# Loading the last four w2 blocks as 112 lines over all engines and 16 lines over four of them

## The chip, the cores and the metric

One core of a Trainium2 chip runs the whole program. The metric is device time in microseconds (us) per execution, the median of several. A profile of one execution comes with each kernel; its times count from the start of its span, which is 1.2 to 1.4 us shorter than the device time.

Throughout, a *line* is one of the 128 partitions of the on-chip memory, and an *engine* without a name is one of the 16 DMA engines. The trace gives them no numbers; where a text names engines 0 to 3, 0 and 1 or 1, or says how many lines each engine carries, that is the author's assumption.

## The reference, cut to what matters

A decoding step of a transformer block with a batch of 2: modulation from `c @ w_mod`, attention of 32 heads over caches of 32768 keys and values, then an MLP. The kernel moves 178 MB of weights and caches through the core once. The argument here touches only the last product, `h @ w2`:

```python
    def _B_ref(x, w1, b1, w2, b2):
        y = _layernorm(x, axis=-1)
        h = _gelu(jnp.einsum('bsd,df->bsf', y, w1) + b1)
        return jnp.einsum('bsf,fd->bsd', h, w2) + b2          # w2: 3584 x 1024, bf16
    ...
    h = _layernorm(x, axis=-1) * (1 + cb) + sb
    x = x + gb * _B_ref(h, B_w1, B_b1, B_w2, B_b2)
    return x
```

## The kernel before

All large loads are one stream on the sync queue, issued as far ahead as memory is free. The 3584 rows of w2 are 28 blocks of 128 rows, one row per line; a block is 2 KB on each line. They come in five loads. Blocks 16 to 27 are the stationary operand of 8 matmuls each, which add into one PSUM tile; the result follows after two small vector operations, a transposing matmul and a copy.

```python
W2_ITEMS = ((0, 8, 96), (8, 16, 112), (16, 24, 128), (24, 27, 144), (27, 28, 150))  # first, end, offset in KB
... # cut
    w2_v = B_w2.rearrange("(p j) n -> p j n", j=FT)
    for m, (j0, j1, off) in enumerate(W2_ITEMS):
        add(("w2", m), [j1 - j0, DM], w2_v[:, j0:j1, :], off * KB)      # 128 lines each
... # cut
    for g in range(16, FT):
        m, j = w2_of[g]
        it = need("w2", m)
        for k in range(KT8):
            pe(lambda e, ...: e.matmul(psO[:, 2 * k:2 * k + 2], lhsT=w[:, j, k * 128:(k + 1) * 128], rhs=gT[:, g, 0:2],
                                       start=False, stop=(g == FT - 1), skip_group_check=True),
               reads=[it.reg, "gT"], writes=["psO"], ...)
    dve(...)   # times the modulation, plus the residual; then one matmul, one copy, the store
```

## Time and profile before

| kernel before | value |
|---|---|
| device time, median of 6 | 420.06 us (419.93 to 420.28) |
| profiled span | 418.7 us |
| DMA busy on its main queue | 98.8% of 16 engines' span |
| blocks 16 to 23 landed (last of 16 completions) | 413.23 us |
| blocks 24 to 26 landed | 415.12 us |
| block 27 landed | 415.76 us |
| last matmul of block 27 starts | 416.02 us |

The trace has several completions per load: 16 for each load of w2 in the kernel before, and 1, 2, 4, 1 and 8 for the bias loads of 1, 2, 4, 1 and 8 lines. The author reads them as one per engine that took part, so that the spread between them tells how far apart the engines are. One further line of the kernel before is needed later. It is the stretch from 411.2 to 415.2 us: length, busy time of PE, PEld, DVE, ACT and POOL with counts, granted clock, DMA busy share, GB/s.

```profile
411.20:415.20 4.00, 3.67 (x73) 3.50 (x74) 0.00 (x0) 0.00 (x0) 0.00 (x0) 0.50 0.80 330
```

DMA engines were busy for 80% of these 4 us and moved 330 GB/s: a fifth of their time was idle, as some had run out of work (seven completions of block 27, the last load of w2, were in by 414.49).

### The profile page before, as it was taken

The numbers are of one execution on the slowest core, as the hardware profiler recorded it, in microseconds if no ns is written. First come the engines' busy times: TensorE is split into PE (matmuls) and PEld (weight loads), VectorE is DVE, ScalarE is ACT, GpSimd is POOL, SyncE is SP. The second block draws the span as 40 slices with busy tenths as digits, with TensorE's granted clock in tenths as the row PEclk, the third lists the DMA queues.
The fourth block names the chain that finished last, engine by engine and source line by source line (L and its number), as shares of the span: only waits on it lengthen the run. The fifth ranks groups of instructions, "written<-read, shape, count | busy, mean of one in ns | idle before, by whom it ended". The sixth has DMA issues, their size and how long they took to land.

```text
span 418.7 us, 11609 instructions
## 1 busy us (share of the span) xinstructions
PE 291.0 (70%) x5183; PEld 231.3 (55%) x5183; DVE 209.6 (50%) x423; ACT 149.4 (36%) x179; POOL 6.8 (2%) x29
## 2 busy tenths in 40 slices
PE   1407449766996895699369957976995699564536
PEld 1104219762993794299149926962894399221214
DVE  1201105546677676467726664766477567620411
ACT  2000015533565364256405632643365166400100
POOL 3000000000000000000000000000000000000000
PEclk9999557986896997799589958986697889576585
DMA  9989999999999999999999999999999999899995
GB/s 373 450 380 449 448 404 493 398 406 446 441 432 429 423 451 429 419 454 457 391 435 476 407 416 448 438 438 426 438 438 426 416 460 457 377 448 428 424 427 249
DMA packets 5581, 178.42 MB, mean 426 GB/s; under 512 B 698, under 2 KB 706, under 8 KB 964
## 3 DMA queue, kind: packets, MB, share of 16 engines
q1 hardware_dynamic: 5572, 178.28, 98.8%
q8 instruction: 8, 0.13, 0.1%
q14 instruction: 1, 0.01, 0.0%
HBM read 178.28 MB, written 0.00 MB: 426 GB/s over the span
## 4 chain that ended last, share of the span: by engine, by line
DMA 71%; PE 24%; DVE 2%; issue 1%; ACT 1%; SPq 1%
DMA V<-in_A_v_cache_dram 39%; DMA wo<-in_A_wo_dram 10%; DMA K<-in_A_k_cache_dram 10%; PE psZ L584 10%; DMA w<-in_B_w_dram 9%; PE psKT L536 8%; DMA wmod<-in_w_mod_dram 4%; PE psS L548 1%; PE psZ L548 1%; PE psS L655 1%; PE psZ L729 1%; PE psZ L469 1%; ACT KT_sb L540 0%; PE psS L469 0%; DVE m1c L553 0%
## 5 line engine op out<-in xcount | busy, mean ns | idle before, releaser
L536 PE MATMUL psKT<-ident,K 128*128 128x128 bf16 x2048 | 163.1, 229 | 11.5 <-DMA K<-in_A_k_cache_dram 11.5
L540 ACT ACTIVATE KT_sb<-psKT 128x1024 bf16<-128x1024 bf16 x96 | 98.2, 1025 | 124.4 <-PE psKT L536 124.4
L542 DVE COPY KT_sb<-psKT 128x1024 bf16<-128x1024 bf16 x160 | 106.7, 688 | 61.6 <-PE psKT L536 61.2
L536 PEld LDWEIGHTS psKT<-ident,K 128*128 128x128 bf16 x2048 | 126.7, 102 | 13.0 <-DMA K<-in_A_k_cache_dram 12.7
L584 PE MATMUL psZ<-V,E_sb 128*32 128x512 bf16 x512 | 46.4, 541 | 23.2 <-DMA V<-in_A_v_cache_dram 20.0
L548 PE MATMUL psS<-qcur,KT_sb 128*128 128x8 bf16 x1024 | 44.7, 167 | 2.2 <-issue 2.2
L584 PEld LDWEIGHTS psZ<-V,E_sb 128*32 128x32 bf16 x512 | 18.7, 130 | 47.7 <-issue 38.8
L548 PE MATMUL psZ<-qcur,KT_sb 128*128 128x8 bf16 x1024 | 43.0, 167 | 2.2 <-issue 1.5
L548 PEld LDWEIGHTS psS<-qcur,KT_sb 128*128 128x128 bf16 x1024 | 40.0, 97 | 2.3 <-issue 2.3
L548 PEld LDWEIGHTS psZ<-qcur,KT_sb 128*128 128x128 bf16 x1024 | 37.9, 96 | 3.4 <-issue 1.6
L572 ACT ACTIVATE E_sb<-S_sb 128x512 bf16<-128x512 f32 x32 | 19.5, 630 | 29.6 <-DVE S_sb L570 29.6
L570 DVE TENSOR_TENSOR S_sb<-S_sb,gmb 128x512 f32<-128x512 f32 x32 | 20.0, 685 | 0.3
L576 DVE TENSOR_REDUCE rs<-E_sb 128x8 f32<-128x512 bf16 x32 | 19.7, 675 | 0.0
L469 PE MATMUL psS<-wmod,inT 128*32 128x512 bf16 x32 | 5.1, 624 | 16.2 <-DMA wmod<-in_w_mod_dram 16.2
L553 DVE TENSOR_REDUCE m1c<-psZ 128x8 f32<-128x512 f32 x16 | 11.1, 693 | 10.2 <-ACT S_sb L552 10.1
L595 DVE RECIPROCAL rinv<-psM 128x1 f32<-128x1 f32 x8 | 1.3, 168 | 27.7 <-PE psM L593 27.7
L605 PE MATMUL psM<-msum,hmat 128*128 128x128 f32 x16 | 4.2, 347 | 13.3 <-DVE msum L600 13.3
L559 PE MATMUL psM<-identf,m 128*8 128x128 f32 x16 | 4.3, 369 | 13.1 <-DVE m L556 13.1
L553 DVE TENSOR_REDUCE m1c<-psS 128x8 f32<-128x512 f32 x16 | 11.1, 693 | 3.2 <-ACT S_sb L552 3.1
L552 ACT ACTIVATE S_sb<-psZ 128x512 f32<-128x512 f32 x16 | 9.5, 595 | 7.5 <-PE psZ L548 7.5
L477 DVE COPY S_sb<-psS 128x512 f32<-128x512 f32 x1 | 0.7, 690 | 22.9 <-PE psS L469 22.9
L469 PEld LDWEIGHTS psS<-wmod,inT 128*32 128x32 bf16 x32 | 1.1, 132 | 19.3 <-DMA wmod<-in_w_mod_dram 18.0
(123 smaller groups left out, 167.5 us busy)
## 6 DMA issues: line engine op xcount, KB each, us to landing
K<-in_A_k_cache_dram SPq DMA_DIRECT2D x16, 4096.0 KB, 27.1
wq<-in_A_wq_dram SPq DMA_DIRECT2D x2, 4096.0 KB, 44.8
wo<-in_A_wo_dram SPq DMA_DIRECT2D x2, 4096.0 KB, 39.0
w<-in_B_w_dram SPq DMA_DIRECT2D x2, 3584.0 KB, 32.5
wmod<-in_w_mod_dram SPq DMA_DIRECT2D x1, 6144.0 KB, 29.8
w<-in_B_w_dram SPq DMA_DIRECT2D x3, 2048.0 KB, 37.8
wmod<-in_w_mod_dram SPq DMA_DIRECT2D x1, 4608.0 KB, 15.8
wmod<-in_w_mod_dram SPq DMA_DIRECT2D x1, 1536.0 KB, 6.0
```

Source lines behind the costliest of these rows:

```text
L469: pe(lambda e, w=it.view, k=k, kk=kk, ch=ch, n=n, q=q: e.matmul(bank[n][32 * q:32 * q + 32, :], lhsT=inT[:, k, :], rhs=w[:, kk, ch * 512:( ...
L536: pe(lambda e, kq=kq, jj=jj, w=kt, t=t: e.transpose(psKT[kq][:, jj * 128:(jj + 1) * 128], w[:, t, :], ident[:, :]), reads=[it.reg, "ident" ...
L540: act(lambda e, src=src: e.activation(KT_sb[g8][:, :, :], src, ACT.Copy), reads=[f"psKT{kq}"], writes=[f"KT_sb{g8}"], sem=f"ev{cc}_{g8}")
L542: dve(lambda e, src=src: e.tensor_copy(KT_sb[g8][:, :, :], src), reads=[f"psKT{kq}"], writes=[f"KT_sb{g8}"], sem=f"ev{cc}_{g8}")
L548: pe(lambda e, t=t, jj=jj: e.matmul(ps[:, t * HPG:(t + 1) * HPG], lhsT=KT_sb[g8][:, jj, :], rhs=qcur[:, :], start=True, stop=True), reads= ...
L552: act(lambda e: e.activation(Sc, ps.rearrange("p (t h) -> p h t", h=HPG), ACT.Copy), reads=[preg], writes=[f"S_sb_{cc}"], sem=f"sc{cc}")
L553: dve(lambda e: e.tensor_reduce(m1c[:, :, cc], ps.rearrange("p (t h) -> p h t", h=HPG), AX.X, ALU.max), reads=[preg], writes=[f"m1c{cc}"])
L559: pe(lambda e: e.matmul(psM[0:HPG, 0:128], lhsT=m1[:, :], rhs=identf[:, :], start=True, stop=True), reads=["m1", "identf"], writes=["psM"])
L570: dve(lambda e: e.tensor_tensor(Sc, Sc, gmb[:, :].unsqueeze(2).to_broadcast([128, HPG, TPC]), ALU.subtract), reads=[f"S_sb_{cc}", "gmb"], ...
L572: act(lambda e: e.activation(Ec, Sc.rearrange("p h (u t) -> p u h t", t=4), ACT.Exp, scale=SCALE), reads=[f"S_sb_{cc}"], writes=[f"E_sb_{c ...
L576: dve(lambda e: e.tensor_reduce(rs4[:, :, cc], Ec.rearrange("p u h t -> p h u t"), AX.XY, ALU.add), reads=[f"E_sb_{cc}"], writes=[f"rs4_{c ...
L584: pe(lambda e, t4=t4, tg=tg, q=q: e.matmul(psO[32 * q:32 * q + 32, :], lhsT=E_sb[:, tg // 4, :, :].rearrange("p h t -> p (h t)"), rhs=vt[: ...
```

## The change

At the end of the stream seven or eight of the 16 engines finish 1.3 us ahead of the rest. In the kernel before, the packets of the eight instruction fetches lasted 881 to 960 ns each, and after the sixth, seventh and eighth of them six, seven and eight completions of a load came about 1.3 us behind the early ones, to the end of the run. The change wants to hand four engines more lines and all others fewer. The last four blocks are loaded with 112 lines; that each engine then carries 7 instead of 8 is the author's count. The remaining 16 lines, with all four blocks (8 KB per line), come as five small loads of 4, 4, 4, 2 and 2 lines.

```diff
-W2_ITEMS = ((0, 8, 96), (8, 16, 112), (16, 24, 128), (24, 27, 144), (27, 28, 150))
+W2_ITEMS = ((0, 8, 96), (8, 16, 112), (16, 24, 128))
+W2_END = ((24, 27), (27, 28))
+W2_LINES = 112
+W2_REST = ((112, 116), (116, 120), (120, 124), (124, 126), (126, 128))
+W2_AT = 144
 ...
+    j0 = W2_END[0][0]
+    w2e = nc.alloc_sbuf_tensor_at("w2e", [128, FT - j0, DM], BF16, offset=abase + W2_AT * KB)
+    for m, (l0, l1) in enumerate(W2_REST):
+        add(("w2r", m), [FT - j0, DM], w2_v[l0:l1, j0:FT, :], W2_AT * KB, slot="w2r", view=w2e[l0:l1, :, :])
+    for m, (ja, jb) in enumerate(W2_END):
+        add(("w2e", m), [jb - ja, DM], w2_v[0:W2_LINES, ja:jb, :], (W2_AT + 2 * (ja - j0)) * KB, view=w2e[0:W2_LINES, ja - j0:jb - j0, :])
 ...  # the loads of w2 no longer wait for one another, as the last ones share a buffer (cut)
 ...  # the matmuls of blocks 24 to 27 read w2e and wait for its load and for the five small ones
```

More of the change, by code (lines that the diff above doesn't have):

```diff
@@ L333, in bass_adaLN_cond__gqa_block_cached__mixer_channel_mlp__decode_kernel, with add @@
     KB = 1024
-    def add(key, shape, src, off, slot=None):
+    def add(key, shape, src, off, slot=None, view=None):
         it = Item()
@@ L341, in add @@
         it.sem = f"d_{slot or it.reg}"
-        it.view = views.get(slot)
+        it.view = views.get(slot) if view is None else view
         if it.view is None:
@@ L383, in need @@
             cur = stream[pos[0]]
-            old = [o.reg for o in stream[:cur.n] if o.off < cur.off + cur.nbytes and cur.off < o.off + o.nbytes]
+            old = [o.reg for o in stream[:cur.n] if not (o.key[0][:2] == cur.key[0][:2] == "w2") and o.off < cur.off + cur.nbytes and cur.off < o.off + o.nbytes]
             if len(cur.view.shape) == 3:
@@ L725, in bass_adaLN_cond__gqa_block_cached__mixer_channel_mlp__decode_kernel @@
     for g in range(16, FT):
-        m, j = w2_of[g]
-        it = need("w2", m)
+        if g in w2_of:
+            m, j = w2_of[g]
+            it = need("w2", m)
+            w, regs = it.view, [it.reg]
+        else:
+            m = 0 if g < W2_END[0][1] else 1
+            it = need("w2e", m)
+            w, j, regs = w2e, g - W2_END[0][0], [it.reg] + [by_key["w2r", n].reg for n in range(len(W2_REST))]
         for k in range(KT8):
-            pe(lambda e, w=it.view, g=g, j=j, k=k: e.matmul(psO[:, 2 * k:2 * k + 2], lhsT=w[:, j, k * 128:(k + 1) * 128], rhs=gT[:, g, 0:2],
+            pe(lambda e, w=w, g=g, j=j, k=k: e.matmul(psO[:, 2 * k:2 * k + 2], lhsT=w[:, j, k * 128:(k + 1) * 128], rhs=gT[:, g, 0:2],
                                                             start=False, stop=(g == FT - 1), skip_group_check=True),
-               reads=[it.reg, "gT"], writes=["psO"], mark=(k == KT8 - 1 and g in (23, 26, 27)))
+               reads=regs + ["gT"], writes=["psO"], mark=(k == KT8 - 1 and g in (23, 26, 27)))
     dve(lambda e: e.tensor_tensor(mT[:, :, :], psO[:, 0:16].rearrange("p (k b) -> p k b", b=2), mod(5), ALU.mult), reads=["psO", "modT"], writes=["mT"])
```

## The prediction

Passages are cut from the recorded text, because no trace or run of this case shows what they say: which engine carries which line, where lines lie in the memory, and the sums of the second rival, which rest on that. What the text came to: without sharing, +0.07 to +0.1 us; for the second rival 422.5 us, with block 24's data 2.5 us later in the middle, or 421.2 us for half of it. The 20% for "about 421", the 30% for "about 422.5" and the middle of 420.8 cannot be followed from what stands: they are the author's estimates. "Port" is the author's name for a place where engines get in each other's way. That PE is quicker at a full clock, as the first rival says, the kernel before shows: eight psKT matmuls took 0.87 us at a granted clock of 0.50 (from 85.13 us) and 0.47 us at 1.00 (from 88.33 us). For the 0.4 us there the text gives no sum.

> **What bounds the kernel now.** I read the page first: the DMA engines carry 98.8% of the span in one queue, and the chain that ended last is 71% DMA and 24% PE. The whole kernel is a stream of loads; compute only shows where a load has just landed.
>
> ```profile
> DMA  9989999999999999999999999999999999899995
> q1 hardware_dynamic: 5572, 178.28, 98.8%
> q8 instruction: 8, 0.13, 0.1%
> w<-in_B_w_dram SPq DMA_DIRECT2D x3, 2048.0 KB, 37.8
> w<-in_B_w_dram SPq DMA_DIRECT2D x1, 768.0 KB, 39.4
> w<-in_B_w_dram SPq DMA_DIRECT2D x1, 256.0 KB, 39.5
> ```
>
> The reader is to see that the engines are full until the last fortieth of the span, and that the two loads which the change touches (768 and 256 KB, blocks 24 to 26 and block 27) are issued 39 us before they land: their issue time is hidden.
>
> Then the chain of waits in order of time, from 405 us on (start, length, what):
>
> ```profile
> 375.40 37.83 DMA w<-in_B_w_dram
> 413.23 0.05 issue
> 413.27 1.87 PE psZ L729 x64
> 415.14 0.03 issue
> 415.17 1.03 PE psZ L729 x32
> 416.20 0.02 issue
> 416.22 0.19 DVE mT L732
> ```
>
> So the end is set in two steps. The load of blocks 16 to 23, which the change leaves alone, lands at 413.23 and lets 64 matmuls go. In the list of single matmuls these start 26.7 ns apart, the last at 414.98. The next would start at 415.00, but blocks 24 to 26 land at 415.12 and it starts at 415.17. **The wait for the changed loads costs 0.17 us.** Block 27 lands at 415.76; its first matmul starts at 415.84 and did not wait. Behind the last matmul stand 2.5 us of DVE, PE and the store that no load touches.
>
> Last, the stretches between those landings (PE, PEld, DVE, ACT, POOL busy, granted clock, DMA share, GB/s), and the DMA rate from 405 to 416 us in 40 slices of 0.275 us:
>
> ```profile
> 408.36:413.23 4.87, 3.77 (x24) 2.25 (x24) 0.69 (x1) 0.00 (x0) 0.00 (x0) 0.50 0.98 417
> 413.23:415.12 1.89, 1.85 (x64) 1.78 (x64) 0.00 (x0) 0.00 (x0) 0.00 (x0) 0.50 0.69 279
> 415.12:415.76 0.64, 0.61 (x23) 0.59 (x23) 0.00 (x0) 0.00 (x0) 0.00 (x0) 0.50 0.07 26
> GB/s 357 536 238 596 298 596 357 417 536 179 655 238 596 238 596 298 536 417 238 655 238 596 201 573 298 499 380 313 402 387 358 387 380 231 194 171 186 45 0 0
> ```
>
> In the last 1.6 us half of the engines are done: the rate halves. The trace's semaphore record says how: of block 27's 16 completions, seven come from 414.11 to 414.49, one at 415.01, eight from 415.47 to 415.76. Each of the 8 instruction fetches (16 KB each) puts one engine back by 1.2 to 1.4 us: before the fetch at 407.08 us eight engines were early, after it seven. The change is aimed at these 1.3 us.
>
> [...] the one-line bias load has one completion from a DMA engine (360.82 us), the two-line one two. [...] one engine alone moves 16384 bytes in 0.611 us, 26.8 GB/s[...].
>
> **The change part by part.**
> *Issue.* Five more DMA issues at 0.43 us (the issues of this group take 327 to 433 ns): 2.2 us on the sync queue, at 376 us, over 30 us ahead of the landing. Cost 0.
> *Waits.* The first matmul of block 24 waits for two semaphores instead of one; some tens of ns at most, an estimate from the 0.05 us of issue in the chain. The queue order (small loads before the 112-line ones) does not delay blocks 16 to 23, which stand ahead of both.
> *Bytes per engine.* Packets of 6144, 2048 and 16384 bytes take 234, 84 and 611 ns; between them one of 8192 takes about 0.31. A line of the two end loads costs 0.318. Engines 0 and 1 get 7 x 0.318 + 5 x 0.31 = 3.78 instead of 8 x 0.318 = 2.54: 1.23 later. Engines 2 and 3: 7 x 0.318 + 3 x 0.31, 0.61 later. The other twelve: 0.32 earlier.
> *Where those engines stand.* Following the packets from the small bias loads [...] to the end, each packet starting where the one before ended, I put the ends of their last data at 413.85, 414.20, 413.95 and 414.71; the eight late engines end at 415.17 to 415.44, none of them 0 to 3. An estimate, as packets carry no engine number. After the change: 415.08, 415.43, 414.55, 415.32, and the late eight 414.85 to 415.12. **The last data come at 415.43 instead of 415.44**: engine 1 takes the place of the late ones. The first three blocks and the rest are complete at about 415.43 - 7 x 0.084 = 414.84 instead of 415.44 - 8 x 0.084 = 414.77, so block 24 starts 0.07 us later.
> *Sum without port sharing:* +0.07 to +0.1 us. The best that any spreading could do is to take away the wait for block 24, -0.17 us, since PE is then busy from 413.27 on.
>
> **The rivals.**
> 1. *It works as meant* (engines 0 to 3 earlier than I place them, fetches elsewhere): at most -0.17 us, 419.87; -0.4 us at the very most if the granted clock is full in the tail, where PE would be quicker and the landing counts. For it: the early engines are just the ones that get more. Against: the PE chain.
> 2. *Ports become the bound.* [...] blocks 16 to 23 can suffer too, which moves all of PE. [...]
> 3. *A wait moves:* PE waits at block 27 or on the small loads' semaphore. Within the sums above.
>
> **Range and chances.** About 45% for no visible port effect (419.8 to 420.2), 20% for part of it (about 421), 30% for all (about 422.5), 5% for a gain beyond 0.2 us. I put the middle at 420.8 and the range at 419.6 to 422.8. Two per cent are 8.4 us: nothing here reaches that.
>
> **What would show it.** Step by step: the chain should still begin its tail at 413.2 to 413.3 with the load of blocks 16 to 23. If ports are free, the 112-line packets last 234 and 84 ns as before and block 24 starts within 0.1 us of 415.2. If ports bind, packets of 8192 bytes last well over 0.31 us, 6144 ones over 234 ns, and a wait of 1 to 3 us stands ahead of the last 32 matmuls. The early seven completions of the last load should close up on the late eight. I am wrong if blocks 16 to 23 themselves land at another time, if the instruction fetches fall on other engines[...].

## The result, and the profile after

| | before | after |
|---|---|---|
| device time, median of 6 | 420.06 us | 422.37 us (422.21 to 422.58) |
| profiled span | 418.7 us | 421.1 us |
| blocks 16 to 23 landed | 413.23 us | 415.64 us |
| five small loads landed | - | 415.68 us |
| blocks 24 to 26 landed | 415.12 us | 417.57 us |
| block 27 landed | 415.76 us | 418.00 us |

The ratio is 1.0055, with a 95% interval of 1.0042 to 1.0068. The intervals of all runs but one (dup_own_port, below) lie clear of 1.

The change costs 2.3 us. The chain of waits of the changed kernel, from 405 us on:

```profile
377.81 39.76 DMA w2e<-in_B_w_dram
417.57 0.05 issue
417.62 1.02 PE psZ L745 x32
418.64 0.02 issue
418.66 0.18 DVE mT L748
```

From 417.57 on it is the old tail, 2.45 us later. The chain names only the load that ended last. PE's own timeline shows the other one (start, length, the instruction, and in brackets the idle time before it), first of the kernel before, where all 96 matmuls stand in one line, then of the changed kernel:

```profile
413.27 2.91 PE L729 MATMUL psZ<-gT,w 128*128 128x2 bf16 x96 [0.30 <-DMA w<-in_B_w_dram]
```

```profile
415.68 1.87 PE L745 MATMUL psZ<-gT,w 128*128 128x2 bf16 x64 [2.54 <-DMA w<-in_B_w_dram]
417.62 1.01 PE L745 MATMUL psZ<-gT,w2e 128*128 128x2 bf16 x32
```

PE idled 2.54 us, in place of 0.30, for blocks 16 to 23, **which the change does not touch**. When its 64 matmuls for them were through, at about 417.41, the wait for the changed loads had only 0.2 us left. Two waits of nearly the same length lie on top of each other, and mending either alone would leave most of the loss.

Where the time goes is in the stretch view of the changed kernel:

```profile
411.20:415.20 4.00, 1.87 (x8) 1.78 (x8) 0.02 (x1) 0.00 (x0) 0.00 (x0) 0.50 0.96 219
```

Against the kernel before, the DMA engines are **busier** (0.96 for 0.80) and move **less** (219 for 330 GB/s). They do not lack work: most packets take longer. The durations of single packets in the trace say so. Before, every packet of 6144 and of 2048 bytes lasted 234 and 84 ns, without exception. After, 93 of the 112 packets of 6144 bytes lasted over 244 ns (mean 369, longest 579), the 16 packets of 8192 bytes of the small loads lasted 309 to 732 ns (mean 566), and 17 packets of 16384 bytes lasted 773 to 1535. These last belong to the untouched load of blocks 16 to 23, whose packets had lasted 611 ns; they start from 411.55 us on, just when the packets of the changed loads begin (411.46).

The lengths of packets do not hold the whole loss. The last data packet of blocks 16 to 23 ended at 414.57, 1.64 us later than before (412.94), but the last completion came 1.06 us after it instead of 0.29. So about a third of the delay lies between the last data packet and its completion; no data packet of this load fills it, and what does was not followed up.

### The profile page after: what moved, and what is told of

Same layout as the page of the kernel before. It is cut to its first block, busy times and chain, and to the rows that moved or that the text cites. A ratio compares the mean times of both kernels' runs of the same rounds, so it can differ in the third digit from the quotient of the medians. Undisturbed runs are those within 1.5% of the kernel's fastest.

```text
span 421.1 us, 11615 instructions
## 1 busy us (share of the span) xinstructions
PE 291.4 (69%) x5183; PEld 233.5 (55%) x5183; DVE 209.9 (50%) x423; ACT 149.5 (36%) x179; POOL 6.8 (2%) x29
## 4 chain that ended last, share of the span: by engine, by line
DMA 71%; PE 23%; DVE 2%; issue 2%; ACT 1%; SPq 1%
DMA V<-in_A_v_cache_dram 38%; DMA K<-in_A_k_cache_dram 10%; DMA wo<-in_A_wo_dram 10%; DMA w2e<-in_B_w_dram 9%; PE psZ L594 9%; PE psKT L546 8%; DMA wmod<-in_w_mod_dram 4%; PE psS L558 1%; PE psZ L558 1%; PE psS L665 1%; SPq L399 1%; PE psZ L479 1%; ACT KT_sb L550 0%; DVE m1c L563 0%; DVE S_sb L580 0%
## 5 line engine op out<-in xcount | busy, mean ns | idle before, releaser
L546 PE MATMUL psKT<-ident,K 128*128 128x128 bf16 x2048 | 166.1, 231 | 12.2 <-DMA K<-in_A_k_cache_dram 12.1
L546 PEld LDWEIGHTS psKT<-ident,K 128*128 128x128 bf16 x2048 | 129.2, 103 | 13.8 <-DMA K<-in_A_k_cache_dram 13.3
L594 PE MATMUL psZ<-V,E_sb 128*32 128x512 bf16 x512 | 44.5, 524 | 20.5 <-DMA V<-in_A_v_cache_dram 17.2
L665 PE MATMUL psS<-wo,atT 128*32 128x512 bf16 x64 | 7.1, 625 | 8.3 <-DMA wo<-in_A_wo_dram 8.3
L487 DVE COPY S_sb<-psS 128x512 f32<-128x512 f32 x1 | 0.7, 692 | 23.3 <-PE psS L479 23.3
L674 DVE COPY S_sb<-psS 128x512 f32<-128x512 f32 x2 | 1.4, 692 | 21.8 <-PE psS L665 14.7
## 6 DMA issues: line engine op xcount, KB each, us to landing
K<-in_A_k_cache_dram SPq DMA_DIRECT2D x16, 4096.0 KB, 26.7
```

The costliest lines, as they stand in the source:

```text
L546: pe(lambda e, kq=kq, jj=jj, w=kt, t=t: e.transpose(psKT[kq][:, jj * 128:(jj + 1) * 128], w[:, t, :], ident[:, :]), reads=[it.reg, "ident" ...
L594: pe(lambda e, t4=t4, tg=tg, q=q: e.matmul(psO[32 * q:32 * q + 32, :], lhsT=E_sb[:, tg // 4, :, :].rearrange("p h t -> p (h t)"), rhs=vt[: ...
L665: pe(lambda e, w=it.view, m=m, j=j, hf=hf, q=q: e.matmul(psS[0][32 * q:32 * q + 32, :], lhsT=atT[m][:, j, :], rhs=w[:, j, hf * 512:(hf + 1 ...
```

## The experiments

**The theory.** In the shapes tried here several engines get in each other's way over the lines that they write, and share what passes there. This was the author's supposition. The recorded texts call it the port theory, and the names of the runs speak of own and same ports; no trace or run of this case shows ports, which lines would share one, or which engine writes which line, so these are names here and no more. **The rivals:** the bytes per engine (by the author's count two engines carry 12 lines instead of 8); and a fixed cost of five more loads and their semaphore.

The figures of all runs, packets from the trace, landings as the last completion of each load:

| run | median us | before beside it | blocks 16 to 23 landed | last of what block 24 waits for | mean ns of 8192 / 6144 bytes | longest ns of 8192 / 6144 |
|---|---|---|---|---|---|---|
| before | 420.06 | | 413.23 | 415.12 | - / 234 | - / 234 |
| the change | 422.37 | 420.06 | 415.64 | 417.57 | 566 / 369 | 732 / 579 |
| dup_same_port | 422.21 | 420.10 | 415.20 | 417.15 | 574 / 336 | 753 / 695 |
| dup_own_port | 420.35 | 420.10 | 413.40 | 415.62 | 309 / 234 | 309 / 234 |
| only_112 | 421.66 | 420.10 | 414.76 | 416.70 | - / 366 | - / 680 |
| two_halves | 422.77 | 420.10 | 414.72 | 417.73 | - / 377 | - / 474 |
| rest_own_port | 422.02 | 420.06 | 414.75 | 417.04 | 471 / 357 | 620 / 633 |
| rest_spread | 422.10 | 420.06 | 414.65 | 416.94 | 500 / 346 | 620 / 480 |
| rest_last | 423.79 | 420.06 | 415.69 | 418.87 | 503 / 429 | 900 / 852 |

### The small loads, to neighbouring lines or to lines four apart

```diff
 # against the changed kernel, both runs
-W2_LINES = 112
+W2_LINES = 128
+    w2d = nc.alloc_sbuf_tensor_at("w2d", [128, FT - j0, DM], BF16, offset=abase + (W2_AT + 8) * KB)
     for m, (l0, l1) in enumerate(W2_REST):
-        add(("w2r", m), ..., view=w2e[l0:l1, :, :])
 # dup_same_port: lines 112 to 115, 116 to 119 ...
+        add(("w2r", m), ..., view=w2d[l0:l1, :, :])
 # dup_own_port: lines 0, 4, 8, 12; 1, 5, 9, 13; 2, 6, 10, 14; 3, 7; 32, 36
+        add(("w2r", m), ..., view=w2d[s:s + 4 * (l1 - l0 - 1) + 1:4, :, :])    # s = 0, 1, 2, 3, 32
```

Both load 128 lines of the last blocks as the kernel before does, and fetch 128 KB a second time with the small loads, into memory that nothing reads. Lines four apart were chosen by the author's assumption of which engine writes which line in a 128-line load, which is not shown. The runs differ in the lines written, and in the time to issue the small loads (252 to 332 ns each, or 562 to 697 with lines four apart), which is over 30 us ahead of their landing.

> The two end loads are 128 lines again, as before the change; the five small loads stay, but fetch the same bytes a second time into a spare buffer, to the same lines 112 to 127 [...]. Port theory: [...] packets of 8192 bytes last clearly over 0.31 us (0.5 and more on average), blocks 16 to 23 land up to 1 us late, and the end comes 2.8 to 3.5 us later than in the kernel before. Byte theory (only the bytes per engine count): engines 0 and 1 carry 1.55 us more, end 0.3 us later than before. Fixed cost of five small loads: the same as in the next run, whatever it is.

> As the run ahead of it, same bytes, same engines, same five small loads, but their lines are four apart in the spare buffer (0, 4, 8, 12 and so on)[...]. Port theory: packets of 8192 bytes last 0.31 us, the 128-line packets 234 and 84 ns, end 0.2 to 0.4 us later than before (engine 1 then ends about 1.55 us later than it did). Byte theory: the same 0.3 us. Fixed cost theory: as slow as the run ahead. [...]

Measured: 422.21 us (ratio 1.0052, interval 1.0035 to 1.0069) and 420.35 us (1.0005, 0.9988 to 1.0021). Same bytes, same number of loads and waits; the lines alone make 1.86 us, where the record had expected about 3 us, or 0. With lines four apart the packets of 8192 bytes all last 309 ns, and those of the large loads 234 and 84 as before. With neighbouring lines the mean is 574. The stretch from 411.2 to 415.2 us again, first with neighbouring lines, then with lines four apart:

```profile
411.20:415.20 4.00, 1.83 (x8) 1.74 (x8) 0.00 (x0) 0.00 (x0) 0.00 (x0) 0.50 0.98 226
```

```profile
411.20:415.20 4.00, 3.59 (x72) 3.50 (x72) 0.00 (x0) 0.00 (x0) 0.00 (x0) 0.50 0.86 355
```

The reader is to see a busy share of 0.98 with 226 GB/s against 0.86 with 355. So the fixed cost of five small loads and of their wait is not what costs: the second run has them too, and with 13 lines on two engines, by the author's count, it is 0.25 us behind, which its interval does not tell from nothing. The sizes in the first run were misses: the end was to come 2.8 to 3.5 us later and came 2.1 later, while blocks 16 to 23 were to land up to 1 us late and landed 1.97 late.

### The 112-line loads alone

```diff
-    for m, (l0, l1) in enumerate(W2_REST):
-        add(("w2r", m), ...)
 ...
-            w, j, regs = w2e, g - W2_END[0][0], [it.reg] + [...]
+            w, j, regs = w2e[0:W2_LINES, :, :], g - W2_END[0][0], [it.reg]
 ...                                        # and rhs=gT[0:112, ...] for blocks 24 to 27
```

The kernel leaves 64 of 3584 products out of each sum and is wrong; the comparison with the reference passed within its tolerance all the same, which says nothing for it.

> The 112-line loads alone: no small loads, and the last 32 matmuls contract over 112 lines (a wrong result on purpose). Each engine carries 7 lines in place of 8. Port theory with 7 neighbouring lines per engine: these packets last over 234 ns (some 300 on average), blocks 16 to 23 land 0.5 to 1.2 us late, end 1.0 to 1.6 us later than before. Byte theory: 0.32 us less for every engine, end 0.17 us earlier (the wait ahead of block 24 goes). If the small loads alone are to blame: the same 0.17 us earlier.

Measured: 421.66 us, 1.56 us later than before (ratio 1.0038, 1.0022 to 1.0055), within the 1.0 to 1.6 of the theory, though these loads bring an eighth **less** (112 lines of 128). Packets of 6144 bytes last 366 ns on average, where some 300 were expected, and blocks 16 to 23 landed 1.53 us late, where 0.5 to 1.2 were. The bytes per engine fall as an explanation with this run. Its stretch:

```profile
411.20:415.20 4.00, 2.27 (x23) 2.18 (x24) 0.00 (x0) 0.00 (x0) 0.00 (x0) 0.50 0.94 235
```

Busy 0.94 with 235 GB/s: the signature needs no small load.

### The same bytes, in two halves

```diff
-        add(("w2e", m), [jb - ja, DM], w2_v[0:W2_LINES, ja:jb, :], ..., view=w2e[0:W2_LINES, ...])
+        for hf in range(2):
+            add(("w2e", m, hf), [jb - ja, DM], w2_v[64 * hf:64 * hf + 64, ja:jb, :], ..., view=w2e[64 * hf:64 * hf + 64, ...])
```

> Each end load is two loads of 64 lines: every engine carries 4 + 4 lines, the same bytes as before the change, over all 16 engines. Port theory: [...] packets of 6144 bytes last up to 0.47 us in place of 0.234, end 1.4 to 2.1 us later than before. Byte theory and fixed cost theory: two more DMAs, end within 0.2 us of before.

Measured: 422.77 us, 2.67 later (ratio 1.0067, 1.0051 to 1.0084), more than the 1.4 to 2.1 expected. The loads bring exactly the bytes of the kernel before, and yet it is slower than the change itself. The longest packet of 6144 bytes lasted 474 ns, 2.03 times 234, which would fit two engines that share evenly what passes one alone; that they did was not shown. 110 of 128 were over 244 ns.

### Can the change be mended by choosing the lines?

```diff
 # rest_own_port
-W2_REST = ((112, 116), (116, 120), (120, 124), (124, 126), (126, 128))
+W2_REST = ((0, 13), (1, 14), (2, 15), (3, 8), (11, 16))          # each with a step of 4 lines
 # and the 112-line loads take lines 16 to 127
 # rest_spread
+W2_REST = ((112, 125), (113, 126), (114, 127), (115, 120), (123, 128))   # each with a step of 4 lines
```

> The change with one part mended: the five small loads really fetch their 16 lines, but these are lines 0 to 15, four apart (0, 4, 8, 12; 1, 5, 9, 13; 2, 6, 10, 14; 3, 7; 11, 15)[...]; the 112-line loads take lines 16 to 127. Port theory: 8192-byte packets mostly at 0.31 us again, but the 112-line packets stay long; end 1.3 to 2.0 us later than before, so 0.3 to 1.0 us earlier than the change as given and close to the 112-line loads alone (1.56 measured). If the small loads' sharing alone made the loss: within 0.3 us of before. [...]

> The change with lines 112 to 127 again in the small loads, but four apart (112, 116, 120, 124 and so on)[...]. Port theory: [...] 8192-byte packets between 0.31 and 0.62 us, end 1.8 to 2.5 us later than before, a few tenths better than the change at most. If four neighbouring lines in one load were the cause by themselves [...]: as the run ahead of it.

Measured: 422.02 and 422.10 us, 1.96 and 2.04 us later than the kernel before (intervals 1.0033 to 1.0067 and 1.0034 to 1.0067). Both come out 0.3 us better than the change, and they cannot be told apart: whether the small loads meet each other or the other loads was not separated by this pair. In the first the packets of 8192 bytes did not go back to 309 ns as expected, but to a mean of 471; I did not follow packet by packet why. What is shown is that the small loads' lines are worth 0.3 us beside the 112-line loads.

### The order

```diff
-    for m, (l0, l1) in enumerate(W2_REST):          # moved below the two 112-line loads
-        add(("w2r", m), ...)
     for m, (ja, jb) in enumerate(W2_END):
         add(("w2e", m), ...)
+    for m, (l0, l1) in enumerate(W2_REST):
+        add(("w2r", m), ...)
```

> The change with the five small loads behind the 112-line ones instead of ahead. Port theory: blocks 16 to 23 land as with the 112-line loads alone (about 1.5 us later than before, where the change had 2.4), but the small loads, which block 24 waits for, end last; end 2.2 to 3.2 us later than before. If only what stands ahead in the queue matters: blocks 16 to 23 land at 413.2 as before in either order.

Measured: 423.79 us, 3.73 later, beyond the 2.2 to 3.2 expected. Blocks 16 to 23 landed at 415.69 us although only 112-line loads stood right behind them. Fourteen of their completions were in by 414.81, one came at 415.08 and one at 415.69; in the 112-line run the last was 414.76. So the expected 1.5 us holds for most engines, not for the last. The last data packet of the load had ended at 413.83, before the small loads' first packet began (415.25); why its completion came 1.86 us later stays open. The rival, that only what stands ahead in the queue matters, would have had 413.2.

No run points to a version better than the kernel before. Its own last matmul starts 0.26 us after the last landing, and PE does not wait in between: the last two matmuls of block 26 and the eight of block 27 start 26.7 ns apart there.

## Why the prediction was right or wrong

The time came out at 422.37 us, inside the range of 419.6 to 422.8 but 1.6 us over its middle. The range was wide enough to hold all three rivals, so being inside it says little. The second rival of the prediction, that engines get in each other's way, is the one that the runs fit (the lines alone made 1.86 us), though not the place that it supposed, which no run shows. Its figure for that case, 422.5, is off by 0.1; it had a chance of 30%.

- **What bounds the kernel.** Right. The tail behind the last matmul did not change: 2.5 us in both traces.
- **Issue and waits cost nothing.** Right. The seven issues for the last blocks took 253 to 427 ns each and were through at 378.6 us; with five small loads and their wait beside packets of the old length, dup_own_port was 0.25 us slower in all.
- **The queue order "does not delay blocks 16 to 23, which stand ahead of both".** This is the step that failed, in the sum without port sharing and in the last part, where the chain was to resume at 413.2 to 413.3. They landed 2.41 us late, and the prediction's own sign "I am wrong if blocks 16 to 23 themselves land at another time" came true. In dup_own_port blocks 16 to 23 landed at 413.40, so standing ahead was enough there; in dup_same_port, where they landed at 415.20, it was not. By the theory an early engine, through with its own share, begins the new loads and gets in the way of a late one; what the trace shows of it is that the long packets of the load ahead start at 411.55, and the packets of the changed loads at 411.46. The second rival named the delay and gave it no number of its own. It carries 2.2 of the 2.4 us by itself, since with blocks 16 to 23 at 415.64 PE cannot reach block 24 before 417.4.
- **The bytes per engine, +0.07 to +0.1 us without sharing.** The run dup_own_port supports the method: 8192 bytes take 309 ns there, and 1.55 us more on two engines (five such packets, by the author's count) came with 0.25 us at the end where 0.2 to 0.4 was expected. For the change itself it is not what sets the time.
- **Where those engines stand.** Right as far as this run shows: its 8192-byte packets form four rows 0.31 us apart that begin at 411.51, 411.58, 411.60 and 412.50, so none of the engines that carry them is among the late eight, which ended their part of blocks 16 to 23 at 412.66 to 412.94 in the kernel before.
- **The size of the sharing.** By the second rival's estimate, block 24's data were to come 2.5 us later in the middle; they came 2.45 later. But the parts were off: with four engines sharing, 8192 bytes were to take 1.2 us (about four times the 0.31 of one), and the longest such packet lasted 732 ns; the 112-line loads alone already cost 1.56 us. For other shapes the time lay 0.5 to 0.7 us outside the expected range, below it in one (dup_same_port) and above it in two (halves, order), so the close hit is partly luck.
- **The chances.** 45% for no visible effect was too much. I weighed sharing as a mere possibility because the loads of w2's last blocks in the trace before had shown none: their packets of 6144 and 2048 bytes all lasted 234 and 84 ns.
- **What was to be seen.** The long packets came as said. The wait of 1 to 3 us did not stand ahead of the last 32 matmuls but ahead of the first 64. The completions of block 27 did not close up: four came from 415.87 to 416.19, twelve from 417.23 to 418.00.

What stays open: the trace has no engine numbers, so that the 112-line loads give each engine 7 *neighbouring* lines is an assumption and is not shown. That the lines make a difference is shown (1.86 us in the pair); the place where the engines meet, and which lines would share it, is not. Two rivals were not tested. The pair reads the same rows of w2 in both runs, so reading cannot make its difference; for the loads of 112 and 64 lines nothing separates reading from writing. And no run had other lines four apart beside 128-line loads, so the pair alone does not separate the step of the lines from which lines they are; with lines 112 to 127 four apart beside 112-line loads the packets of 8192 bytes stayed long (mean 500 ns).

## What to carry to other kernels

Count the engines, but also ask which lines they write. In these runs the 6144-byte packets kept their 234 ns in loads of 128 lines, in the kernel before and with small loads to lines four apart beside them. 112 lines alone (366 ns on average) and twice 64 (377) did not keep it, nor did the 128 lines with small loads to neighbouring lines beside them (336). Levelling the engines at the end of this stream by giving some of them more lines cost 2.3 us in all, and the load ahead, on which the compute was waiting, paid first: it landed 2.41 us late. In the profile, a DMA busy share that rose (0.80 to 0.96) while GB/s fell (330 to 219) was the sign of it: look at the duration of single packets of one size, and at the time from a load's last packet to its last completion.
